# Three early loads of an attention kernel: issued from ScalarE's queue instead of SyncE's

## The chip, the cores and the metric

The kernel runs on one core of a Trainium2 chip. A core has a matrix engine (TensorE, PE in the profile, with its weight loads as PEld), three engines that work on tiles (VectorE or DVE, ScalarE or ACT, GpSimd or POOL) and SyncE (SP), which here only issues transfers between HBM and the on-chip memory. The engines run their own instruction streams and wait for one another through semaphores. The transfers are carried out by 16 DMA engines that all the queues share. The metric is the device time of one execution in microseconds, and the median of several runs is compared.

## The reference

```python
B, Sq, D = 8, 112, 640
H, Sk, Dh = 32, 512, 192
q = (x @ wq).reshape(B, Sq, H, Dh).transpose(0, 2, 1, 3)
scores = einsum("bhqd,bhkd->bhqk", q, k_cache) * Dh ** -0.5
p = softmax(scores, axis=-1)
o = einsum("bhqk,bhkd->bhqd", p, v_cache)
out = o.transpose(0, 2, 1, 3).reshape(B, Sq, H * Dh) @ wo
```

All arrays are bfloat16. `x` is 8 x 112 x 640 (1.15 MB), `wq` is 640 x 6144, `wo` 6144 x 640, and each cache is 8 x 32 x 512 x 192 (50 MB), so that some 117 MB have to be read.

## The kernel before

The work is cut into 64 units: 8 groups of 4 heads, and within a group the 8 batches. For each unit TensorE makes the scores of 4 heads (`do_S`, L949), ScalarE the exponentials (L1047), TensorE the products with v (`do_PV`, L967), VectorE and ScalarE normalise (L1112 to L1115, L1054), TensorE transposes the result (`do_T`, L978) and ScalarE stores it as the left side of the output projection (L1064). Between these, in slots that a table `slot` gives to each unit, TensorE makes the query projection of the next group and the output projection of the last one (`do_pair`, L928 and its helper L858).

Keys come as they lie in memory and are turned by VectorE in 32 x 32 blocks (`do_KT`, L1106), two units ahead. Three of every four value blocks are copied by GpSimd into a tile with a column of ones (`middle`, L1209). Query weights need another order of columns; GpSimd makes it (`reorder`, L1202). On GpSimd both stand in one list, written out by hand: for each unit first the weight chunk that is due, then a check of the softmax sums, then the copy of the values two units ahead.

The head of the program matters here. TensorE starts with 31 matmuls on zeros (`WARM`, L984 and L858), and then transposes `x` in 128-row blocks: `do_X(m)`, L854, five matmuls for each block. `x` is loaded in three pieces (`XM`): blocks 0 and 1, blocks 2 and 3, blocks 4 to 6; `do_X(0)` waits for the first piece, `do_X(2)` for the second, `do_X(4)` for the third. VectorE evacuates blocks 0 and 2 and part of 3 (L1134), ScalarE block 1 and the rest of 3 (L1023). Eight more matmuls on zeros (`BRIDGE`, L990 and L858) lie between the transposes and the first query projection. That one, `do_Q0_first` (L872), makes three column blocks of the first half of the rows and goes through the five 128-row chunks of the first query weights in order, waiting for each one's own semaphore `mW0[dc]`. Then come a fourth block (L892) and two blocks that read GpSimd's reordered copy (`do_Q0`, L887), blocks 4 to 6 of `x`, and the first unit's scores.

All loads are issued by SyncE in one list (`on_sync`), in this order: first piece of `x`, second piece of `x`, the five chunks of the first query weights (`load_wq(0, dc)`), keys of unit 0 (four transfers), third piece of `x`, and then keys, the second group's query weights, values and output weights. A load waits for its buffer where one is used again: three for keys, four for values. The issue of all loads is one line, L1309. ScalarE issues no loads. Its first instruction is the load of the table of activation functions (L1019, `ACT_TABLE_LOAD`), then a dummy exponential on one column, and then the evacuation of block 1 of `x`.

Of the kernel before, what the change touches and what calls it, by code (L numbers as in the profile page):

```python
# [666 lines left out]
def build_main(nc, x, k_cache, v_cache, wq, wo, out, flag, regs, hints):  # L667
    B, SQ, D = x.shape
    _, H, SK, DH = k_cache.shape
# [17 lines left out]
    WARM, WN, BRIDGE, RAW = 30, 25, 8, 4  # L687
    HINT_AT = {"act": 55, "dve": 54, "pool": 40, "sp": 56}
    NM = 2
    KP = [4] * NU  # L690
    PRE = 2 * 6
    EARLY_LOADS = ("k1", "q", "v0", "k2", "v1", "k3", "v2", "o")
# [68 lines left out]
    with ExitStack() as es:  # L761
# [58 lines left out]
        def W(eng, s, v):  # L820
            if v > 0:
                eng.wait_ge(s, v)
# [24 lines left out]
        def on_tensor(pe):  # L847
# [166 lines left out]
                do_pair(i, 1)  # L1014
            get_flag(pe)

        def on_scalar(act):
            W(act, vI, 1)
            act.activation(dmy[:, 1:2], dmy[:, 0:1], ACTF.Exp)  # L1019

            def evac_x(m, n=DC):
                W(act, pXT, m + 1)
                act.activation(xT[:, 0:n, 128 * m:128 * (m + 1)],  # L1023
                               psb[:, m, 0:128 * n].rearrange("p (c s) -> p c s", c=n), ACTF.Copy).then_inc(aX, 1)

            def evac(g, c, h):
                n = q_index[g, c, h]
                W(act, pQ, n + 1)
                if g >= 2 and c == 0 and h == 0:
                    W(act, pS, 4 * B * (g - 1))  # L1030
                act.activation(qT[g % 2][:, c, HQ * h:HQ * (h + 1)], ps[:, bank_of_Q0(n) if g == 0 else 6 + h, 0:HQ],  # L1031
                               ACTF.Copy).then_inc(aQ, 1)

            def evac_pair(i, j):
                if slot[i, j] and slot[i, j][0][0] == "Q" and slot[i, j][1] != FRONT:
                    for h in range(2):
                        evac(*slot[i, j][0][1:], h)

            def exp(u, a):
                W(act, pS, 4 * u + a + 1)  # L1040
                if a == 3 and u >= 2:
                    W(act, gM, u + 1)
                if a == 0:
                    W(act, pPV, u - 1)
                    if u < 2:
                        W(act, gV, 1)
                act.activation(pT[u % 2][:, a, :, 0:SQ], ps[:, a, 0:4 * SQ].rearrange("p (t q) -> p t q", t=4), ACTF.Exp,  # L1047
                               scale=scale).then_inc(aEX, 1)

            def norm(u):  # L1050
                W(act, vRC, u + 1)
                W(act, pT_, u - 1)
                for e in range(2):
                    ins = act.activation(os_[u % 2][:, DH * (2 + e):DH * (3 + e)], pv_of(u)[0:SQ, 1, e, 0:DH], ACTF.Copy,  # L1054
                                         scale=rinv[:, u % 4, 2 + e:3 + e])
                ins.then_inc(aNM, 1)

            def tevac(u):
                g, b = divmod(u, B)
                W(act, pT_, u + 1)  # L1060
                if g > 0:
                    W(act, pO, 2 * (MT * (g - 1) + (SQ * b + SQ - 1) // 128 + 1))
                src = psb[:, bank_of_T(u), 2:2 + 4 * RW].rearrange("p (k w) -> p k w", k=2)[:, :, 0:3 * SQ]
                act.activation(oT[:, :, SQ * b:SQ * (b + 1)].rearrange("p (k c) q -> p k c q", k=2),  # L1064
                               src.rearrange("p k (c q) -> p k c q", c=3), ACTF.Copy).then_inc(aT, 1)

            evac_x(1)
            evac_x(3, 2)
            for c in range(6):
                evac(0, c, 0)  # L1070
            for m in (4, 5):
                evac_x(m)
            for c in range(6):
                if c < 4:
                    exp(0, c)
                evac(0, c, 1)
            for i in range(1, NU + 2):
                if i == HINT_AT["act"]:
                    hints[mybir.EngineType.Activation] = act.mark_branch_hint_location()
                if i < NU:  # L1080
                    exp(i, 0)
                if i >= 2:
                    tevac(i - 2)
                if i < NU:
                    exp(i, 1)
                evac_pair(i, 0)
                if i < NU:
                    exp(i, 2)
                    exp(i, 3)
                if 1 <= i <= NU:  # L1090
                    norm(i - 1)
                evac_pair(i, 1)
            get_flag(act)
# [143 lines left out]
        def on_sync(sp):  # L1237
            loads = []

            def add(dst, src, s, count, waits):  # L1240
                loads.append((dst, src, s, count, waits))

            def load_x(j):
                m0, m1 = XM[j]
                add(xs[:, m0:m1, :], x.rearrange("b s d -> (b s) d")[128 * m0:128 * m1].rearrange("(m p) d -> p m d", p=128),
                    mX[j], 16, [])

            def load_wq(g, dc):
                src = wq[128 * dc:128 * (dc + 1), 4 * DH * g:4 * DH * (g + 1)]
                if g == 0:  # L1250
                    add(wqs[:, 0, dc, :], src, mW0[dc], 16, [])
                else:
                    add(wqr[:, dc, :], src, mWQ[dc], 16 * g, [(gW, DC * (g - 2) + dc + 1)])

            def load_wo(g, k):
                r0 = 4 * DH * g + 256 * k
                src = wo[r0:r0 + 256].rearrange("(p e) d -> p e d", e=2)
                for e in range(2):
                    add(wos[:, g % 2, 2 * k + e, :], src[:, e], mWO[g % 2][k], 32 * (g // 2 + 1),
                        [(pO, 2 * MT * (g - 1))])  # L1260

            def load_k(u):
                g, b = divmod(u, B)
                src = k_cache[b, 4 * g:4 * g + 4].rearrange("a (j s) d -> (a j) (s d)", s=16)
                for h in range(KP[u]):
                    cs = slice(16 // KP[u] * DH * h, 16 // KP[u] * DH * (h + 1))
                    add(kr[u % NK][:].rearrange("p s d -> p (s d)")[:, cs], src[:, cs], mK[u % NK], 16 * sum(KP[u % NK:u + 1:NK]),
                        [(vKT, 4 * (u - NK + 1))])

            def load_v(u):  # L1270
                g, b = divmod(u, B)
                for a in range(4):
                    add(vs[u % NV][:, a, 32:32 + 4 * DH], v_cache[b, 4 * g + a].rearrange("(m t) d -> m (t d)", t=4),
                        mV[u % NV], 64 * (u // NV + 1), [(pPV, u - NV + 1)])

            load_x(0)
            load_x(1)
            for dc in range(DC):
                load_wq(0, dc)
            load_k(0)  # L1280
            load_x(2)
            for step in EARLY_LOADS:
                for c in step[1:]:
                    {"k": load_k, "v": load_v}[step[0]](int(c)) if step[0] in "kv" else None
                if step[0] == "q":
                    for dc in range(DC):
                        load_wq(1, dc)
                if step[0] == "o":
                    for c in range(3):
                        load_wo(0, c)  # L1290
            for u in range(4, NU + 1):
                if u < NU:
                    load_k(u)
                if u - 1 >= 3:
                    load_v(u - 1)
                for g in range(2, NG):
                    d = u - max(4, 8 * (g - 1) - 6)
                    if 0 <= d < DC:
                        load_wq(g, d)
                for g in range(1, NG):  # L1300
                    d = u - (8 * g - 1)
                    if 0 <= d < 3:
                        load_wo(g, d)
            for n, (dst, src, s, count, waits) in enumerate(loads):
                if n == len(loads) - HINT_AT["sp"]:
                    hints[mybir.EngineType.SP] = sp.mark_branch_hint_location()
                for ws, wv in waits:
                    W(sp, ws, wv)
                sp.dma_start(dst, src).then_inc(s, 16)  # L1309
            parts = [(m, 0, D) for m in range(MT - 1)] + [(MT - 1, 0, HL), (MT - 1, HL, D)]  # L1310
            for n, (m, d0, d1) in enumerate(parts):
                W(sp, vO, 2 * (MT * (NG - 1) + m + 1) - (d1 == HL))
                sp.dma_start(out.rearrange("b s d -> (b s) d")[128 * m:128 * (m + 1), d0:d1], ob[:, m, d0:d1]).then_inc(mOUT[n], 16)
            get_flag(sp)
            for n in range(len(parts)):
                sp.wait_ge(mOUT[n], 16)
# [53 lines left out]
```

## Time and profile before

| what | value |
|---|---|
| median of 5 runs | 393.25 us (391.98 to 394.67) |
| the profiled execution's own time | 393.61 us |
| its span, first to last instruction | 391.9 us |
| TensorE busy | 386.1 us (99%) |
| VectorE, ScalarE, GpSimd busy | 283.8, 250.4, 152.7 us |
| read from HBM | 117.54 MB |
| moved by the DMA engines, mean | 306 GB/s |

The profile is of one execution. Its page gives the busy time of each engine, the span in 40 slices, and groups of instructions; the trace behind it answers for lines, waits and windows. A row of the timeline begins with the start and the duration in microseconds, then the engine, the line of the kernel, the operation, what it writes and reads, and how many instructions were merged; in brackets stands how long the engine was idle before and what ended that. A row of SyncE tells when transfers were issued, not when they landed. The DMA engines' share in the windows can be a little over 1, since packets overlap.

### The profile page before, as it was taken

Reading aid. Unit: us, or ns where it says so; the run is one execution under the profiler, and the core shown is the slowest. Engines: PE = TensorE matmul, PEld = TensorE weight load, DVE = VectorE, ACT = ScalarE, POOL = GpSimd, SP = SyncE. Lnnn points to the kernel's source line nnn. Section 1 sums busy time; section 2 is a strip of 40 time slices with the busy share of each in tenths; the row PEclk is TensorE's granted clock in tenths of the full one; section 3 lists DMA queues with packets and bytes.
Section 4 is the critical chain, followed back from the end, with each engine's and each line's share of the span. In section 5 each row is a group of like instructions: output and inputs, shape, how many; then the busy total and the mean of one; then the engine's idle time right before and its main releaser. Section 6 shows DMA issues by size and latency. Waiting matters only on the chain.

```text
span 391.9 us, 19834 instructions
## 1 busy us (share of the span) xinstructions
PE 386.1 (99%) x8865; PEld 243.2 (62%) x8262; DVE 283.8 (72%) x506; ACT 250.4 (64%) x550; POOL 152.7 (39%) x352
## 2 busy tenths in 40 slices
PE   8999988999999999999999999999999999999997
PEld 4555664756666656666665666665666666667664
DVE  1664786787896777776787766876778776789935
ACT  2767764766656765657746667557665667657662
POOL 5542444343443354334352354332553232333331
PEclk9999999999999999999999999999999999999999
DMA  8999999999999999989999999989899799999912
GB/s 268 377 362 317 331 330 355 348 363 333 331 358 366 319 315 355 296 281 300 329 344 310 283 318 318 345 283 309 263 335 333 229 302 302 321 302 293 304 48 70
DMA packets 88584, 120.00 MB, mean 306 GB/s; under 512 B 9776, under 2 KB 88496, under 8 KB 88496
## 3 DMA queue, kind: packets, MB, share of 16 engines
q1 hardware_dynamic: 88496, 118.72, 91.0%
q8 instruction: 68, 1.11, 1.2%
q14 instruction: 20, 0.16, 0.1%
HBM read 117.54 MB, written 1.15 MB: 303 GB/s over the span
## 4 chain that ended last, share of the span: by engine, by line
PE 96%; issue 1%; DMA 1%; POOL 1%; DVE 0%; ACT 0%; SPq 0%
PE ps L967 22%; PE ps L858 22%; PE ps L928 21%; PE ps L949 21%; PE ps L978 6%; PE ps L887 2%; PE ps L854 1%; DMA xs<-in_x_dram 1%; PE ps L872 1%; DMA vs<-in_v_cache_dram 0%; POOL vm L1209 0%; PE ps L892 0%; POOL wqs L1202 0%; DVE kt L1106 0%; DVE acc L1126 0%
## 5 line engine op out<-in xcount | busy, mean ns | idle before, releaser
L1106 DVE STREAM_TRANSPOSE kt<-kr 128x384 int32<-128x384 int32 x256 | 195.5, 872 | 12.5 <-DMA kr<-in_k_cache_dram 12.4
L1047 ACT ACTIVATE pT<-ps 128x448 bf16<-128x448 f32 x256 | 131.0, 561 | 84.4 <-PE ps L949 82.2
L949 PEld LDWEIGHTS ps<-qT,kt 32*128 32x128 bf16 x6144 | 77.0, 93 | 29.5 <-issue 20.2
L928 PE MATMUL ps<-wos,oT 128*128 128x320 bf16 (+2 forms) x342 | 92.9, 298 | 0.0
L967 PE MATMUL ps<-vm,pT 128*128 128x193 bf16 x768 | 91.5, 247 | 1.0 <-ACT oT L1064 0.8
L858 PE MATMUL ps<-wos,oT 128*128 128x320 bf16 (+1 forms) x340 | 91.3, 296 | 0.0
L949 PE MATMUL ps<-qT,kt 32*128 32x112 bf16 x6144 | 87.3, 208 | 0.4 <-DVE kt L1106 0.3
L1226 POOL TENSOR_SCALAR bad<-rinv 112x4 f32<-112x4 f32 x64 | 14.6, 228 | 187.1 <-DVE rinv L1112 186.9
L1209 POOL COPY vm<-vs 128x1152 int32<-128x1152 int32 x64 | 73.4, 1147 | 26.8 <-issue 19.9
L967 PEld LDWEIGHTS ps<-vm,pT 128*128 128x128 bf16 x768 | 67.9, 97 | 22.0 <-ACT oT L1064 11.7
L928 PE MATMUL ps<-xT,wqs 128*128 128x448 bf16 (+1 forms) x210 | 73.5, 350 | 1.0 <-POOL wqs L1202 1.0
L858 PE MATMUL ps<-xT,wqs 128*128 128x448 bf16 (+2 forms) x226 | 74.1, 341 | 0.0
L1054 ACT ACTIVATE os<-ps,rinv 112x192 bf16<-112x192 f32 x128 | 47.9, 436 | 26.7 <-DVE rinv L1112 26.7
L967 PE MATMUL ps<-vs,pT 128*128 128x193 bf16 x256 | 62.6, 245 | 0.0
L1031 ACT ACTIVATE qT<-ps 128x448 bf16<-128x448 f32 x96 | 47.8, 554 | 19.4 <-PE ps L928 13.5
L928 PEld LDWEIGHTS ps<-wos,oT 128*128 128x128 bf16 x342 | 33.2, 97 | 43.0 <-issue 35.9
L1129 DVE TENSOR_TENSOR acc<-ps,acc 128x320 f32<-128x320 f32 x84 | 37.3, 486 | 26.1 <-PE ps L928 25.9
L1064 ACT ACTIVATE oT<-ps 128x672 bf16<-128x672 bf16 x64 | 46.4, 725 | 2.1 <-PE ps L978 2.1
L1112 DVE RECIPROCAL rinv<-ps 112x4 f32<-112x4 f32 x64 | 11.1, 174 | 48.7 <-PE ps L967 48.7
L928 PEld LDWEIGHTS ps<-xT,wqs 128*128 128x128 bf16 x210 | 20.4, 97 | 35.4 <-issue 29.1
L1115 DVE TENSOR_TENSOR os<-ps,rinv 112x384 bf16<-112x384 f32 x64 | 35.7, 558 | 7.3 <-DVE rinv L1112 0.5
L1202 POOL COPY wqs<-wqr 128x384 bf16<-128x384 bf16 x70 | 33.2, 506 | 4.9 <-DMA wqr<-in_wq_dram 4.9
(44 smaller groups left out, 156.4 us busy)
## 6 DMA issues: line engine op xcount, KB each, us to landing
kr<-in_k_cache_dram SPq DMA_DIRECT2D x256, 192.0 KB, 4.0
vs<-in_v_cache_dram SPq DMA_DIRECT2D x256, 192.0 KB, 4.0
wos<-in_wo_dram SPq DMA_DIRECT2D x48, 160.0 KB, 4.1
wqr<-in_wq_dram SPq DMA_DIRECT2D x35, 192.0 KB, 4.7
wqs<-in_wq_dram SPq DMA_DIRECT2D x5, 192.0 KB, 4.1
out_dram<-xs SPq DMA_DIRECT2D x6, 160.0 KB, 1.8
xs<-in_x_dram SPq DMA_DIRECT2D x2, 320.0 KB, 3.3
xs<-in_x_dram SPq DMA_DIRECT2D x1, 480.0 KB, 5.9
```

Source lines behind the costliest of these rows:

```text
L858: return pe.add_instruction(mybir.InstMatmult(name=nc.get_next_instruction_name(), engine=mybir.EngineType.PE, ins=[pe.lower_ap_or_imm(rhs ...
L928: mm = (pe.matmul if h == hs[0] and f == 0 else held)(ps[:, bank_of(pair, h), cs], w, rhs[h][:, cs], q == 0, q == n - 1 and f == cuts - 1)
L949: mm = pe.matmul(ps[:, a, SQ * t:SQ * (t + 1)], kt[u % NT][p, t, c // 2, :, c % 2], qT[g % 2][p, c, SQ * b:SQ * (b + 1)], start=(c == 0), ...
L967: mm = pe.matmul(pv[:, k, e, 0:DH + 1], pT[u % 2][:, a, t, :], src[:, a, v0:v0 + DH + 1], start=(t == 0), stop=(t == 3), skip_group_check= ...
L1031: act.activation(qT[g % 2][:, c, HQ * h:HQ * (h + 1)], ps[:, bank_of_Q0(n) if g == 0 else 6 + h, 0:HQ], ACTF.Copy).then_inc(aQ, 1)
L1047: act.activation(pT[u % 2][:, a, :, 0:SQ], ps[:, a, 0:4 * SQ].rearrange("p (t q) -> p t q", t=4), ACTF.Exp, scale=scale).then_inc(aEX, 1)
L1054: ins = act.activation(os_[u % 2][:, DH * (2 + e):DH * (3 + e)], pv_of(u)[0:SQ, 1, e, 0:DH], ACTF.Copy, scale=rinv[:, u % 4, 2 + e:3 + e])
L1064: act.activation(oT[:, :, SQ * b:SQ * (b + 1)].rearrange("p (k c) q -> p k c q", k=2), src.rearrange("p k (c q) -> p k c q", c=3), ACTF.Co ...
L1106: dve.transpose(dst, src).then_inc(vKT, 1)
L1115: dve.tensor_tensor(os_[u % 2][:, 0:2 * DH].rearrange("p (e d) -> p e d", e=2), pv[0:SQ, 0, :, 0:DH], rinv[:, u % 4, 0:2][:, :, None].broa ...
L1129: ins = dve.tensor_tensor(ob[:, m, cs] if g == NG - 1 else acc[:, m, cs], src, acc[:, m, cs], op=ALU.add)
L1209: gp.tensor_copy(vm[u % NM][:].rearrange("p a (t w) -> p a t w", w=RW)[:, :, :, 0:DH].bitcast(I32), vs[u % NV][:, :, 32:32 + 3 * DH].rearr ...
```

## The change

ScalarE issues three of the loads at its very start, ahead of the table load: the second piece of `x` (320 KB) and chunks 1 and 3 of the first query weights (192 KB each). SyncE's list loses these three; it now begins with the first piece of `x`, chunks 0, 2 and 4, the keys of unit 0. Two helper functions give the source of a piece and of a chunk. Semaphores, sizes, destinations and the waits of those who read the data are the same, and TensorE's, VectorE's and GpSimd's instructions keep their order.

```diff
+    ACT_W0 = (1, 3)
...
+        def x_piece_src(j):
+            m0, m1 = XM[j]
+            return x.rearrange("b s d -> (b s) d")[128 * m0:128 * m1].rearrange("(m p) d -> p m d", p=128)
+
+        def wq_src(g, dc):
+            return wq[128 * dc:128 * (dc + 1), 4 * DH * g:4 * DH * (g + 1)]
+
         def on_scalar(act):
+            act.dma_start(xs[:, XM[1][0]:XM[1][1], :], x_piece_src(1)).then_inc(mX[1], 16)
+            for dc in ACT_W0:
+                act.dma_start(wqs[:, 0, dc, :], wq_src(0, dc)).then_inc(mW0[dc], 16)
             W(act, vI, 1)
             act.activation(dmy[:, 1:2], dmy[:, 0:1], ACTF.Exp)
...
             load_x(0)
-            load_x(1)
             for dc in range(DC):
-                load_wq(0, dc)
+                if dc not in ACT_W0:
+                    load_wq(0, dc)
             load_k(0)
             load_x(2)
```

More of the change, by code (lines that the diff above doesn't have):

```diff
@@ L1244, in load_x @@
                 m0, m1 = XM[j]
-                add(xs[:, m0:m1, :], x.rearrange("b s d -> (b s) d")[128 * m0:128 * m1].rearrange("(m p) d -> p m d", p=128),
-                    mX[j], 16, [])
+                add(xs[:, m0:m1, :], x_piece_src(j), mX[j], 16, [])
             def load_wq(g, dc):
-                src = wq[128 * dc:128 * (dc + 1), 4 * DH * g:4 * DH * (g + 1)]
+                src = wq_src(g, dc)
                 if g == 0:
```

## Prediction

> **What bounds the kernel now.** I began with the page (span, busy times, DMA row).
>
> ```profile
> span 391.9 us, 19834 instructions
> PE 386.1 (99%) x8865; PEld 243.2 (62%) x8262; DVE 283.8 (72%) x506; ACT 250.4 (64%) x550; POOL 152.7 (39%) x352
> ...
> DMA  8999999999999999989999999989899799999912
> ```
>
> TensorE is busy 386.1 of 391.9 us, so a change at the head can only matter through TensorE's few idle moments. The DMA row is as full as TensorE's, so the second question is whether transfers pace TensorE anywhere. The list of waits of TensorE over the whole span has five entries, all short; besides the two shown (who, for whom: us, times, longest) there are 1.0 us before the first warm-up matmul, 0.3 for a key transpose at 55 us and 0.2 for x:
>
> ```profile
> PE ps L928 <- POOL wqs L1202: 1.0, 1, 1.0
> PE ps L967 <- ACT oT L1064: 0.8, 1, 0.8
> ```
>
> Then the head, in order of time (start, duration, engine, line):
>
> ```profile
> 0.73 1.28 ACT L1019 ACT_TABLE_LOAD   x1 [0.73 <-PEq L1355]
> 0.74 0.95 SPq L1309 DMA_DIRECT2D xs<-in_x_dram  x2
> 1.74 2.36 SPq L1309 DMA_DIRECT2D wqs<-in_wq_dram  x5
> 3.93 2.29 PE L854 MATMUL ps<-ident,xs 128*128 128x128 bf16 x20 [0.17 <-DMA xs<-in_x_dram]
> 5.19 0.70 ACT L1023 ACTIVATE xT<-ps 128x640 bf16<-128x640 bf16 x1 [2.96 <-PE ps L854]
> 5.91 4.54 POOL L1202 COPY oT<-wqs 128x384 bf16<-128x384 bf16 x10 [3.50 <-DMA wqs<-in_wq_dram]
> 6.52 2.09 SPq L1309 DMA_DIRECT2D kr<-in_k_cache_dram  x4
> 6.84 3.02 PE L872 MATMUL ps<-xT,wqs 128*32 128x448 bf16 x60
> 8.65 2.89 SPq L1309 DMA_DIRECT2D wqr<-in_wq_dram  x5
> 10.74 2.07 PE L887 MATMUL ps<-xT,oT 128*128 128x448 bf16 x10
> ```
>
> The only transfer that TensorE waits for here is the first piece of x: issued at 0.74, landed 3.05 us later (3.79), transposes from 3.93. The second piece, issued at 1.23, takes 3.5 us to land (4.7). Its ten transposes come behind the first ten, which at 2.29/20 = 0.11 us each last until about 5.0, so nothing waits for it. The five weight chunks, issued 0.47 us apart from 1.74 and landing after 4.0 to 4.1 us, are in by 7.8; the projection (6.84, five steps of 3.02/5 = 0.6 us) wants the last at 9.2, and GpSimd, which starts on the first at 5.91, is through at 10.45, before TensorE's reordered columns at 10.74. **None of the three transfers that move is late today.**
>
> The windows view tells how full the transfers are (the last two numbers: DMA share and GB/s):
>
> ```profile
> 1.50:2.00 0.50, 0.50 (x10) 0.00 (x0) 0.00 (x0) 0.50 (x1) 0.50 (x5) 1.00 0.39 41
> 2.00:2.50 0.50, 0.50 (x10) 0.00 (x0) 0.00 (x0) 0.22 (x2) 0.35 (x8) 1.00 0.67 141
> 2.50:4.00 1.50, 1.33 (x18) 0.10 (x3) 0.00 (x0) 0.00 (x0) 0.00 (x0) 1.00 0.98 352
> 12.00:26.00 14.00, 14.00 (x273) 8.50 (x263) 8.66 (x14) 10.31 (x22) 7.06 (x14) 1.00 1.07 375
> ```
>
> From 2.5 us on the DMA engines are full. SyncE's own rows run end to start from 0.74 to 66 us, never more than 0.45 us apart, so up to there its stream waits for no buffer and hence not for TensorE. Where does that stream meet TensorE? In the chain between 58 and 67 us:
>
> ```profile
> 59.48 1.47 DMA vs<-in_v_cache_dram
> 60.95 3.56 issue
> 64.51 1.15 POOL vm L1209
> 65.65 0.91 POOL wqs L1202 x2
> 66.61 0.36 PE ps L928
> ```
>
> A piece of v issued at 59.48 lands 4.9 us later (64.4). GpSimd, idle till then, copies it (1.15), reorders a weight chunk (0.91), and only then TensorE goes on at 66.61, after the 1.0 us wait listed above. The chain's link from that piece back to a value product at 59.34 is an inference I do not follow: the buffer was freed by the fifth product, at about 48.6. So at 66.6 us the schedule is set by transfers and TensorE has **1.0 us in hand**. After that it shows no wait that the list counts.
>
> **The change, part by part.**
>
> *Off SyncE's queue:* three issues, (1.74 - 1.23) + 2 x 0.47 = 1.45 us. First weight chunk up by 0.51 us, third by 0.98, fifth and everything behind by 1.45. But the transfers were full already, and SyncE shows it: four k issues at 6.52 take 2.09 and five at 8.65 take 2.89, 0.52 and 0.58 each against 0.47 in the first weight rows. It is being held back. Being ahead only brings it to that brake sooner; the bytes ahead of any later piece stay the same. Bounds for the stream: later by nothing that a row shows, earlier by at most 1.45 us. I take 0, by the nearest row (share 0.98 to 1.07). What two queues might win is the ramp: 0.5 us at 141 instead of 352 GB/s and 0.5 at 41 are (211 + 311) x 0.5 / 352 = 0.74 us of transfer at the utmost, and most of that is latency that a second queue has too.
>
> *Onto ScalarE:* three issues at 0.43 to 0.51 each (SyncE's rows; ScalarE has none). Table load 0.73 to about 2.15, done 3.45, dummy exponential (0.20) 3.65; first real work at 5.19. Cost 0; cover 1.5 us. Even at SyncE's slowest early row, 1.06 us, it would end at 0.73 + 3.18 + 1.28 + 0.20 = 5.4, 0.2 late, and the next paragraph moves that work later too. Nobody waits for the dummy.
>
> *The second piece of x now starts with the first.* Both are 320 KB and issued together at 0.74 into full engines. The first piece loses its head start. Bounds for its landing: 3.79 (unchanged, if ScalarE's queue gets going late) and 4.7 (where the second lands now; the two together hold the same bytes). Two equal transfers served in turn end nearly together, so I take 4.5, nearer the upper end: +0.7 us. Transposes, their evacuations and the projection follow with unchanged durations, so TensorE starts the projection at about 7.5 instead of 6.84. [...] No row here shows two load queues at work.
>
> *Weight chunks:* the pairs (0, 1) and (2, 3) arrive together, so the first may land at the second's time, about 0.5 us later (6.3). The projection wants it at 7.5. GpSimd ends at up to 10.95 instead of 10.45, while its reader moves from 10.74 to 11.4. Cost 0; cover 0.45 us, the same as today less 0.05 to 0.3.
>
> *Sum:* TensorE +0.7 us from 4 to 66 us; there it finds 1.0 us of waiting for v, which swallows it: +0.7 - 0.7 + 0 (stream) = 0. The wait shrinks to about 0.3. Profiled execution: 393.6 us (span 391.9 and 1.7 around it), after: 393.6. It stands 0.36 above the median 393.25 of runs that spread over 2.7 us; the forecast against the median is **393.3**. Where the cover would be gone: each further 0.1 us at the head beyond 1.0 costs 0.1.
>
> **Rivals.**
>
> 1. *Slower: the array's full speed comes later.* Matmuls run at half pace first (20 transposes of 128 columns 0.11 us each; later 448 columns in 3.02/15 = 0.20), and the pace steps up just before the projection, some 5.6 us after the first warm-up matmul at 0.99. Warm-up ends at about 3.76 and today leaves a hole of 0.17 us; mine is 0.9. If that restarts the count, full pace comes at about 4.7 + 5.6 = 10.3 instead of 6.6; 3.7 us at half pace lose up to 1.85. Head 0.7 + 1.85 = 2.55, less the 1.0 of cover: +0.2 to +1.5, 394.4 likely. It decides from a head delay over 1.0. For it: the hole lies in the middle of the warm-up. Against: TensorE would still be busy three quarters of that stretch. [...]
> 2. *Faster: the stream keeps part of its 1.45 us.* v lands earlier and the wait at 66 shrinks from both sides: at most -0.3 with a head 0.7 late, at most -1.0 with an unharmed head; 392.6. For it: shares of 0.98 and a DMA rate of 316 GB/s between 26 and 42 us. Against: SyncE's braked rows above.
> 3. *Nothing happens:* ScalarE's issues reach the engines late, x lands as now: 393.3, the same time by another way.
> 4. *Slower: two queues disturb each other* and the stream itself falls behind; every us lost before 64.4 is a us at the end. No row prices it; by the 1.07 against 0.98 share, some 0.5 to 2 us.
>
> **How the numbers follow.** Main case 0.52, rival 1 0.20, rival 2 0.10, rival 3 0.10, rival 4 0.08. Half a per cent is 2.0 us, about what this kernel's measurement tells from none. No case's middle lies beyond it; the upper ends of 1 and 4 and the spread of the runs put 0.14 above, that spread and what I have not seen 0.09 below, 0.77 within. Range: rival 2's end, 392.2, to rival 1's upper end with some spread, 395.0.
>
> **What would show it.** In the changed profile: ScalarE's table load from about 2.2; the first piece of x landing near 4.5 and transposes starting there (right), or at 3.9 (rival 3); projection at 7.5 with five steps of 0.6 (right) or 1.1 (rival 1); TensorE's wait for GpSimd near 66 us at about 0.3 instead of 1.0, ending at the same 66.6. It is wrong if that wait keeps its size or the point moves by over 0.5 us.

## The result

The changed kernel takes 394.38 us, median of 52 runs, against 393.07 for 94 runs of the kernel before. The ratio is **1.0026, with a 95% interval of 1.0016 to 1.0036**: about 1.0 us slower (the medians themselves lie 1.3 us apart; the ratio is not their quotient). The interval leaves out 1, so the loss is real, but it is inside the half per cent that the forecast called no change, and inside its range. But the forecast's likeliest case said 393.3. The time that came is that of its first rival, 394.4, to which it gave 2 chances in 10.

The page of the changed kernel's profile (execution of 394.24 us):

```profile
span 392.5 us, 19834 instructions
...
PE 386.9 (99%) x8865; PEld 243.3 (62%) x8262; DVE 284.2 (72%) x506; ACT 250.3 (64%) x550; POOL 152.8 (39%) x352
...
q1 hardware_dynamic: 87936, 118.00, 90.7%
...
q10 hardware_dynamic: 560, 0.72, 0.5%
```

The new queue, q10, carries 560 packets and 0.72 MB, just the three moved loads. The span grew by 0.6 us from one profiled execution to the other. The head, in order of time:

```profile
0.74 0.49 ACTq L1026 DMA_DIRECT2D xs<-in_x_dram  x1
1.25 0.98 ACTq L1028 DMA_DIRECT2D wqs<-in_wq_dram  x2
2.26 1.28 ACT L1030 ACT_TABLE_LOAD   x1 [2.26 <-issue]
4.84 2.29 PE L855 MATMUL ps<-ident,xs 128*128 128x128 bf16 x20 [1.08 <-DMA xs<-in_x_dram]
7.92 3.91 PE L873 MATMUL ps<-xT,wqs 128*32 128x448 bf16 x60
12.71 2.06 PE L888 MATMUL ps<-xT,oT 128*128 128x448 bf16 x10
```

Three readings. The transposes start at 4.84 instead of 3.93, after a wait of 1.08 us for x (0.17 before). Their duration, 2.29, is the same. But the first projection now takes 3.91 us instead of 3.02, and the reordered columns (L888) start at 12.71 instead of 10.74: the head is **1.97 us** late, 0.91 of it from x and 1.06 from a slower array. The windows show the slower array (columns: window, its length, busy time and count for PE and the others, clock, DMA share, GB/s):

```profile
6.60:9.60 3.00, 3.00 (x33) 1.13 (x28) 0.85 (x2) 0.59 (x2) 3.00 (x8) 1.00 1.07 382
9.80:12.00 2.20, 2.20 (x52) 1.18 (x48) 2.09 (x2) 0.49 (x2) 0.53 (x2) 1.00 1.07 370
26.00:42.00 16.00, 16.00 (x376) 9.77 (x357) 10.07 (x17) 12.31 (x28) 5.95 (x14) 1.00 1.07 372
```

33 matmuls in 3.0 us, then 52 in 2.2. The first window also holds short matmuls from before the projection; the weight loads inside the projection show the step cleanly:

```profile
9.01 0.16 PEld L873 LDWEIGHTS ps<-xT,wqs 128*32 128x32 bf16 x4 [0.22 <-issue]
9.39 0.16 PEld L873 LDWEIGHTS ps<-xT,wqs 128*32 128x32 bf16 x4 [0.22 <-issue]
9.76 1.63 PEld L873 LDWEIGHTS ps<-xT,wqs 128*32 128x32 bf16 x36 [0.22 <-issue]
```

Four of them each 0.37 us, then 36 in a row, four each 0.19. TensorE was busy all the time, at half pace until about 9.8. The clock column stays at 1.00 in both windows, so it cannot be trusted for this stretch; the spacing can. The third line of the windows matters further down: between 26 and 42 us the loads now run at 372 GB/s, where the first profile of the kernel before had 316:

```profile
26.00:42.00 16.00, 16.00 (x386) 9.35 (x361) 9.95 (x16) 12.01 (x28) 4.77 (x11) 1.00 0.99 316
```

And the waits of TensorE over the whole span:

```profile
PE ps L855 <- DMA xs<-in_x_dram: 1.1, 1, 1.1
PE ps L985 <- DVE wt L1107: 1.0, 1, 1.0
PE ps L968 <- ACT oT L1075: 0.8, 1, 0.8
PE ps L950 <- DVE kt L1117: 0.3, 1, 0.3
```

The wait for GpSimd's weights near 66 us, 1.0 us before, is gone. So the sum of the two profiles is +1.97 at the head and -1.37 from there to the end, which is the +0.60 of the span. Compared matmul by matmul, 1.15 us come back exactly where that wait was (the matmul at 66.61 before starts at 67.48, where the one ahead of it is 2.02 late). Another 0.35 come back near 365 us; there the second and third profiles of the kernel before gain as much on the first, so that part belongs to the first profile and not to the change.

### The profile page after: what moved, and what is told of

It is laid out like the page before. It is cut to its first block, busy times and chain, and to the rows that moved or that the text cites. A ratio compares the mean times of both kernels' runs of the same rounds, so it can differ in the third digit from the quotient of the medians.

```text
span 392.5 us, 19834 instructions
## 1 busy us (share of the span) xinstructions
PE 386.9 (99%) x8865; PEld 243.3 (62%) x8262; DVE 284.2 (72%) x506; ACT 250.3 (64%) x550; POOL 152.8 (39%) x352
## 3 DMA queue, kind: packets, MB, share of 16 engines
HBM read 117.54 MB, written 1.15 MB: 302 GB/s over the span
## 4 chain that ended last, share of the span: by engine, by line
PE 97%; DMA 1%; DVE 0%; ACT 0%; issue 0%
PE ps L968 22%; PE ps L859 22%; PE ps L929 22%; PE ps L950 21%; PE ps L979 6%; PE ps L888 2%; DMA xs<-in_x_dram 1%; PE ps L873 1%; PE ps L855 1%; PE ps L893 0%; DVE kt L1117 0%; DVE acc L1137 0%; ACT oT L1075 0%; ACT pT L1058 0%; DVE xs L1140 0%
## 5 line engine op out<-in xcount | busy, mean ns | idle before, releaser
L968 PEld LDWEIGHTS ps<-vm,pT 128*128 128x128 bf16 x768 | 67.9, 97 | 22.1 <-ACT oT L1075 11.6
L1123 DVE RECIPROCAL rinv<-ps 112x4 f32<-112x4 f32 x64 | 11.1, 174 | 51.9 <-PE ps L968 51.9
```

The source lines that it names most:

```text
L968: mm = pe.matmul(pv[:, k, e, 0:DH + 1], pT[u % 2][:, a, t, :], src[:, a, v0:v0 + DH + 1], start=(t == 0), stop=(t == 3), skip_group_check= ...
```

## The experiments

Each ratio below is against runs of the kernel before on the same chip. The theory after this: the second piece of x takes the engines from the first; TensorE stands idle for 1.1 us in the middle of its warm-up; that idle stretch, the hole, puts off the array's full pace; and the delay is only partly taken back later. The rivals: that full pace comes when it comes, and one profile proves nothing; that the weight chunks or the second queue cost by themselves; and, for what is taken back, that the wait near 66 us was chance.

**e1_x_only** is the changed kernel with the piece of x alone moved.

```diff
-    ACT_W0 = (1, 3)
+    ACT_W0 = ()
```

> Of the change only one part: the second piece of x on ScalarE's queue, all five weight chunks back on SyncE's. Theory (x pieces side by side): the first piece lands at about 4.7 as in the changed kernel, TensorE waits 1.1 us for it, the array's full pace comes later in many runs, and the time is the changed kernel's, +0.6 to +1.3 us over before (ratio 1.0015 to 1.0033). Rival (the weight chunks in pairs are what costs): first piece at 3.8 to 4.2 and the time within 0.3 us of before.

Measured: 394.26 us (12 runs), ratio 1.0040 (1.0013 to 1.0067), the changed kernel's loss.

```profile
4.79 2.29 PE L855 MATMUL ps<-ident,xs 128*128 128x128 bf16 x20 [1.03 <-DMA xs<-in_x_dram]
7.87 3.71 PE L873 MATMUL ps<-xT,wqs 128*32 128x448 bf16 x60
```

The first piece landed at 4.65, the hole is 1.0 us, the projection is slow again. The weight chunks are not needed for the loss.

**e4_hole** leaves the loads of the kernel before and only shortens the warm-up, so that the same hole arises.

```diff
-    WARM, WN, BRIDGE, RAW = 30, 25, 8, 4
+    WARM, WN, BRIDGE, RAW = 19, 25, 8, 4
```

> The kernel before, loads untouched, with 20 instead of 31 warm-up matmuls, which leaves the changed kernel's hole of about 1.1 us ahead of the transposes. Theory: full pace comes late as in the changed profile (near 9.7 us or later, half of the projection at half pace), TensorE reaches 54 us 1.0 to 1.8 us later, but the loads land as before, so that its wait near 66 us swallows up to 1.0: time +0.1 to +0.8 us (1.0003 to 1.002). Rival (no effect of the hole): full pace near 6.6, wait near 66 us 1.0 us, time within 0.2 us of before.

Measured: 394.29 us, ratio 1.0035 (1.0009 to 1.0060).

```profile
3.92 2.29 PE L854 MATMUL ps<-ident,xs 128*128 128x128 bf16 x20 [1.08 <-DMA xs<-in_x_dram]
7.00 3.75 PE L872 MATMUL ps<-xT,wqs 128*32 128x448 bf16 x60
```

x is on time, and still the projection takes 3.75 us. A hole alone, with no queue touched, costs as much as the change (the intervals overlap). The median lost more than the 0.1 to 0.8 expected (1.4 us, interval 0.35 to 2.4), so less of the delay is swallowed than I still believed then.

**e3_more_warm** and **e9_changed_warm36** fill the hole in the changed kernel, wholly and by half.

```diff
-    WARM, WN, BRIDGE, RAW = 30, 25, 8, 4
+    WARM, WN, BRIDGE, RAW = 42, 25, 8, 4     # e3_more_warm
+    WARM, WN, BRIDGE, RAW = 36, 25, 8, 4     # e9_changed_warm36
```

> The changed kernel with 43 instead of 31 warm-up matmuls, so that the hole before the first transposes (1.1 us) is filled. Theory (the hole postpones full pace): full pace at the projection's start or before, five steps of 0.6 us; TensorE then is 0.9 us late from x alone and the earlier loads have removed its 1.0 us wait: time within 0.3 us of before, 0.8 to 1.2 us under the changed kernel (ratio to before 0.999 to 1.001). Rival (full pace depends on chance, not on the hole): still +0.7 to +1.3 us over before (1.0018 to 1.0033).

> The changed kernel with 37 instead of 31 warm-up matmuls: half of the hole is filled, some 0.55 us is left. [...] Rival (the loss is the late x alone and grows with its delay): as the changed kernel, since x lands as late.

Measured: 392.56 us, ratio 0.9986 (0.9963 to 1.0008), and 392.83 us, ratio 1.0000 (0.9982 to 1.0018). First e3_more_warm, then e9_changed_warm36:

```profile
4.93 1.50 PE L855 MATMUL ps<-ident,xs 128*128 128x128 bf16 x20 [0.17 <-DMA xs<-in_x_dram]
7.00 3.02 PE L873 MATMUL ps<-xT,wqs 128*32 128x448 bf16 x60
```

```profile
4.87 2.21 PE L855 MATMUL ps<-ident,xs 128*128 128x128 bf16 x20 [0.61 <-DMA xs<-in_x_dram]
7.60 3.02 PE L873 MATMUL ps<-xT,wqs 128*32 128x448 bf16 x60
```

x lands as late as in the changed kernel (4.79 and 4.74), and **the loss is gone**. With the hole filled, full pace comes already during the transposes (1.50 instead of 2.29). With 0.6 us left of it, full pace comes just before the projection, the head is 0.76 us late (reordered columns at 11.50), and the time is that of the kernel before, as the forecast's likeliest case had it. (The interval of e9 reaches 1.0018 and so just touches that of the changed kernel; that of e3 lies below it.) So a hole of 0.6 us was borne and one of 1.0 to 1.1 was not, in the profiles and in the medians.

The moment of full pace, read from the spacing of the matmuls, wanders from profile to profile even without a long hole: in the eleven profiles whose holes are at most 0.7 us it comes between 4.3 us (e5_w_after_x, below) and 6.9 us (e9, and the second profile of the kernel before). In the three with a hole of 1.0 to 1.1 us it comes at 8.5 (e4), 9.3 (e1) and 9.8 (changed). It is the gap between the two groups, and not any single profile, that speaks against the rival of chance.

**e2_w_behind_table** was to move only weight chunks, out of the way of x. Against the changed kernel:

```diff
-            act.dma_start(xs[:, XM[1][0]:XM[1][1], :], x_piece_src(1)).then_inc(mX[1], 16)
+            W(act, vI, 1)
+            act.activation(dmy[:, 1:2], dmy[:, 0:1], ACTF.Exp)
             for dc in ACT_W0:
                 act.dma_start(wqs[:, 0, dc, :], wq_src(0, dc)).then_inc(mW0[dc], 16)
-            W(act, vI, 1)
-            act.activation(dmy[:, 1:2], dmy[:, 0:1], ACTF.Exp)
...
             load_x(0)
+            load_x(1)
```

> The other part alone, and moved so that it cannot touch x: both first pieces of x on SyncE, chunks 1 and 3 issued by ScalarE behind its table load and dummy exponential (from about 2.3 us). Theory that SyncE's issuing paces the loads between 28 and 66 us: SyncE is two issues (0.95 us) ahead, v of unit 8 lands 1 us or more before 64.4, TensorE's 1.0 us wait near 66 us shrinks to 0 to 0.3, x lands at 3.8, and the time is 0.5 to 1.0 us under before (ratio 0.9974 to 0.9987). Rival (the DMA engines pace them, and the earlier landing in the changed profile was chance): wait stays, time within 0.3 us of before.

Measured: 393.87 us, ratio 1.0016 (0.9989 to 1.0044), open either way. It did not do what it was made for:

```profile
0.74 1.28 ACT L1027 ACT_TABLE_LOAD   x1 [0.74 <-PEq L1365]
...
1.01 0.87 ACTq L1029 DMA_DIRECT2D wqs<-in_wq_dram  x2
...
4.38 1.07 PE L855 MATMUL ps<-ident,xs 128*128 128x128 bf16 x10 [0.63 <-DMA xs<-in_x_dram]
...
6.17 0.73 PE L855 MATMUL ps<-ident,xs 128*128 128x128 bf16 x10 [0.72 <-DMA xs<-in_x_dram]
```

The loads stand behind the table load in the program, but were issued at 1.01, while it ran, and so fell among the pieces of x: two holes, 0.63 and 0.72, neither as long as 1.0, and the later transposes at full pace.

**e5_w_after_x** made ScalarE wait for the first piece of x and took chunks 3 and 4, both pieces of x on SyncE. Against the changed kernel:

```diff
-    ACT_W0 = (1, 3)
+    ACT_W0 = (3, 4)
...
-            act.dma_start(xs[:, XM[1][0]:XM[1][1], :], x_piece_src(1)).then_inc(mX[1], 16)
+            W(act, vI, 1)
+            act.activation(dmy[:, 1:2], dmy[:, 0:1], ACTF.Exp)
+            W(act, mX[0], 16)
             for dc in ACT_W0:
                 act.dma_start(wqs[:, 0, dc, :], wq_src(0, dc)).then_inc(mW0[dc], 16)
-            W(act, vI, 1)
-            act.activation(dmy[:, 1:2], dmy[:, 0:1], ACTF.Exp)
...
             load_x(0)
+            load_x(1)
```

> Only weight chunks moved, and without touching x: both first pieces of x on SyncE, ScalarE waits for the first piece's landing and then issues chunks 3 and 4. Theory (x side by side and the hole are the whole loss): first piece lands at 3.8, no wait longer than 0.3 us before the transposes, first projection starts 0.8 us after the last transpose, chunks in before they are read; time within 0.4 us of before (ratio 0.999 to 1.001). Rival 1 (a head start of SyncE's stream is worth something in an ordinary execution): 0.5 to 1.0 us under before (0.9974 to 0.9987). Rival 2 (a second load queue costs by itself): 0.5 to 1.3 us over (1.0013 to 1.0033).

Measured: 394.67 us, ratio 1.0036 (1.0013 to 1.0058). None of the three cases: the chunks came too late.

```profile
3.87 0.86 ACTq L1030 DMA_DIRECT2D wqs<-in_wq_dram  x2
...
9.24 0.75 PE L873 MATMUL ps<-xT,wqs 128*32 128x448 bf16 x12 [1.31 <-DMA wqs<-in_wq_dram]
...
10.68 0.97 PE L873 MATMUL ps<-xT,wqs 128*32 128x448 bf16 x12 [0.69 <-DMA wqs<-in_wq_dram]
```

Issued at 3.87 and 4.29 on an otherwise empty queue, they landed at 9.2 and 10.6, in line with the keys that SyncE had issued at 3.66 and 4.14 (8.3 and 9.8). The trace's packets show where the time went: the first packet of ScalarE's queue starts at 6.54, 2.7 us after its issue (1.65 in the changed kernel). TensorE stood for 2.0 us, and here the windows show the half pace in their clock column too:

```profile
4.30:11.00 6.70, 4.58 (x83) 2.28 (x77) 1.40 (x4) 1.04 (x2) 4.02 (x9) 1.00 0.98 330
11.10:14.40 3.30, 3.30 (x31) 1.21 (x24) 2.75 (x4) 1.96 (x4) 0.54 (x2) 0.50 1.07 382
14.50:20.00 5.50, 5.50 (x130) 3.72 (x129) 3.12 (x5) 3.59 (x7) 4.08 (x10) 1.00 1.07 374
```

An array already at full pace (36 matmuls of the projection in 1.89 us) fell back to half after two holes of 1.3 and 0.7 (0.50 in the clock column from 11.1 to 14.4 us), though it was busy all through that stretch. This is a toll of the same kind as in the changed kernel, seen from the other side. It was recorded in three of the twelve runs only, this one among them (mean clock 0.996), and they are the three slowest.

**e7_before_look2** and **e8_before_look3** are the kernel before, unchanged, profiled twice more.

> The kernel before once more, unchanged, for its profile. Theory (the 1.0 us wait of TensorE for GpSimd near 66 us was in that one execution): no such wait, v of unit 8 lands before 64.0, and the span is the end of the first projection's fifth step plus 381 us. Rival (it belongs to the kernel, and is the cover of the prediction): wait of 0.8 to 1.2 us near 66 us again, span plus 382.

> The same once more. Theory: no wait near 66 us in at least one of the two looks. Rival: the wait in both.

Measured: executions of 392.65 and 394.44 us. The waits of TensorE in the second profile, then the first two lines of the third:

```profile
PE ps L984 <- DVE wt L1096: 1.0, 1, 1.0
PE ps L967 <- ACT oT L1064: 0.8, 1, 0.8
PE ps L949 <- DVE kt L1106: 0.3, 1, 0.3
```

```profile
PE ps L928 <- POOL wqs L1202: 1.3, 1, 1.3
PE ps L984 <- DVE wt L1096: 1.0, 1, 1.0
```

**The wait near 66 us is absent in one profile and 1.3 us in the other.** Both sides of the expectation hold in part: the wait is neither chance in a single execution nor a fixed cover.

**e11_before_warm36, e6_before_warm42, e10_before_warm54** and a repeat, **e12_before_warm42_again**, delay the transposes of the kernel before with a longer warm-up and no hole.

```diff
-    WARM, WN, BRIDGE, RAW = 30, 25, 8, 4
+    WARM, WN, BRIDGE, RAW = 36, 25, 8, 4     # or 42, or 54
```

> The kernel before with 37 warm-up matmuls, which end at about 4.3 at half pace: no hole, transposes 0.2 to 0.4 us later. Theory: the small hole of 0.17 us in the kernel before costs nothing, and the delay is swallowed or regained: within 0.4 us of before (0.999 to 1.001). [...]

> The kernel before, loads untouched, with 43 instead of 31 warm-up matmuls: the transposes start 0.9 us later with no hole ahead of them, as in e3_more_warm, which has the changed loads. [...] Rival (the moved loads are what made e3_more_warm fast): 0.6 us or more slower than e3_more_warm, +0.5 to +1.0 over before.

> e6_before_warm42 once more, on the same chip as the two other warm-up lengths. If its 0.8 us (0.9979) was real: 0.9970 to 0.9990 again, and a look without the late stalls of the first profile. If it was the spread of the runs: within 0.3 us of before.

> The kernel before with 55 warm-up matmuls: TensorE is kept busy until 5.1 to 5.7 us, so the transposes start 1.2 to 1.8 us late without a hole. Theory (head delays come through once the wait near 66 us is used up): GpSimd's reordered columns are reached 0.5 to 1.2 us after those of e6_before_warm42, no wait near 66 us, what follows them 380 us; time +0.2 to +1.0 us over before (1.0005 to 1.0025). Rival (delays at the head are always swallowed): within 0.2 us of before.

Measured: 37 matmuls 392.74 us, ratio 0.9995 (0.9982 to 1.0009); 43 matmuls 392.66, 0.9979 (0.9960 to 0.9998), and again 393.15, 1.0007 (0.9992 to 1.0023); 55 matmuls 393.57, 1.0016 (1.0003 to 1.0030). The gain of the first run with 43 did not come back, so it is no faster version, and e3_more_warm, whose interval holds 1, is none either. Nor does it matter whether loads were moved: filled up with 43 warm-up matmuls, both kernels take about the time of the kernel before. With 55:

```profile
5.55 1.87 PE L854 MATMUL ps<-ident,xs 128*128 128x128 bf16 x20
...
11.89 1.31 PE L887 MATMUL ps<-xT,oT 128*128 128x448 bf16 x6
```

The head is 1.15 us late by this profile (11.89 against 10.74), the median 0.6 us (interval 0.1 to 1.2). Here a head delay without hole or moved loads comes through by about half; how much in one execution depends on stalls such as this one, from the repeat with 43:

```profile
PE ps L928 <- DVE acc L1129: 0.9, 1, 0.9
```

Put together, one profile of each (us; "rest" is the span less the start of the reordered columns; v8 is the landing of the last piece of v of unit 8, its issue plus its time to landing):

| run | first x lands | wait for x | reordered columns start | rest | v8 | ratio |
|---|---|---|---|---|---|---|
| before, three profiles | 3.8, 3.7, 3.8 | 0.2, 0, 0.2 | 10.7, 10.8, 10.4 | 381.1, 380.1, 382.3 | 64.4, 63.4, 64.5 | 1 |
| changed | 4.7 | 1.1 | 12.7 | 379.7 | 61.3 | 1.0026 |
| e1_x_only | 4.7 | 1.0 | 12.5 | 380.1 | 62.8 | 1.0040 |
| e9_changed_warm36 | 4.7 | 0.6 | 11.5 | 379.8 | 61.3 | 1.0000 |
| e3_more_warm | 4.8 | 0.2 | 10.9 | 379.8 | 63.4 | 0.9986 |
| e2_w_behind_table | 4.3 | 0.6 + 0.7 | 11.4 | 379.9 | 63.6 | 1.0016 |
| e5_w_after_x | 3.9 | 0.2 | 13.5 | 380.1 | 61.7 | 1.0036 |
| e4_hole | 3.8 | 1.1 | 11.6 | 380.3 | 64.0 | 1.0035 |
| e11_before_warm36 | 3.8 | 0 | 10.8 | 380.1 | 63.8 | 0.9995 |
| e6, e12 (43) | 3.9, 3.8 | 0, 0 | 10.5, 10.8 | 382.9, 381.3 | 64.1, 63.2 | 0.9979, 1.0007 |
| e10_before_warm54 | 3.8 | 0 | 11.9 | 380.2 | 64.0 | 1.0016 |

In the six profiles with loads moved off SyncE the rest is 379.7 to 380.1, mean 379.9; in the eight without, 380.1 to 382.9, mean 381.0, and only there does TensorE wait for weights or for VectorE's accumulation after 60 us. v8 lands at 62.3 on average with moved loads and at 63.9 without, and between 26 and 42 us the loads run at 363 to 372 GB/s in each of the six and at 316 to 350 in each of the eight. So the moved issues do bring later loads forward, on average by 1.6 us, but by 0.4 to 2.7 in single profiles and not in step with what was moved (0.5 us of issuing in e1, 0.95 in e2 and e5, 1.45 in the others). That this saves about 1 us of late stalls is a tendency only: five of the six also have a late head, and a late head alone takes the wait away (e4 and e10, loads not moved, show none). No run isolated it, since both tries to move the weight chunks alone (e2, e5) failed as tests.

## Why the prediction was right or wrong

*The half per cent and the range:* right. No case was worth 2 us, and none came. The bar is wide, though: the middle of every case that the forecast listed lies inside it, so the bar does not tell them apart, and by the forecast's own sign (the point at 66.6 us moving by over 0.5; it moved by 0.88) the likeliest case was wrong.

*"The second piece of x now starts with the first":* right in kind, and the size was at the upper end that I gave (4.7 measured, 4.5 taken); e1 shows it alone. That the two would be served in turn was my assumption, for which the profile of before had no row; the packets of the trace agree with it: from 3.0 to 6.5 us of the changed profile SyncE's queue moved 618 KB and ScalarE's 673, and from 7 to 9 us of e5's 311 and 315. ScalarE's queue began later (first packets at 2.39 against 1.82, both issued at 0.74), and the first piece landed just ahead of the second (4.71 and 5.01).

*"Onto ScalarE" and "Weight chunks":* right. The table load ran from 2.26 to 3.54, TensorE never waited for a chunk, and e1 without the moved chunks loses as much as the whole change (the intervals overlap). The first chunk even landed at 5.6, not 6.3. One remark there does not come out: a cover of 0.45 us is more than today's 0.29 (10.45 to 10.74), not less; nothing rested on it.

*The pace of the array, put aside into rival 1:* here the likeliest case failed. It had the projection follow "with unchanged durations", and the reason against the rival was "TensorE would still be busy three quarters of that stretch". Three quarters was not enough: with a hole of 1.1 us half pace lasted to about 9.8 and cost 1.06 us. e4 shows the hole alone to be sufficient, and e3 and e9 show that filling it, or half of it, removes the loss. Rival 1 had the mechanism (a long hole puts off full pace: 8.5 to 9.8 us in the three profiles with one, at most 6.9 in the others), the place and the final number, its head delay of 2.55 being 1.97 in the profile. Its count of 5.6 us after the first warm-up matmul was one sample: without a long hole the profiles give 3.3 to 5.9.

*"... earlier by at most 1.45 us. I take 0":* wrong for the loads. The nearest row, braked issues in the first 12 us, was the wrong place to look; the stretch that counts is 26 to 42 us, where the engines moved 316 to 350 GB/s in every profile with the loads left on SyncE and 363 to 372 in every one with loads moved. The rival quoted the 316 and the sum ignored it. v8 landed 3.1 us earlier than in the first profile, 2.8 before the mean of the three (64.1), beyond the bound of 1.45. What sets the rate there was not settled; between 10 and 66 us of the first profile nine of SyncE's issues take 1.1 to 1.8 us instead of 0.43, each starting within 0.4 us of a 16 KB instruction fetch in the trace, and the forecast did not count them. For the time of this profile the 0 did no harm: TensorE came to the point at 66.6 us only at 67.48, when in the first profile too GpSimd was through (66.56).

*"1.0 us in hand":* half right. In the changed profile and in those of e1, e4, e9 and e10, all with a late head, about 1.15 us come back at that point against the first profile, with and without moved loads, as the forecast had reckoned. But the cover was read from one execution. Two more profiles gave waits of 0 and 1.3, so there is not always something to give back, and e4 lost more in the median than a cover of 1.0 would leave (0.9 us late at the head, 1.4 lost, at least 0.35).

So the right total of the first rival came from a head delay that was 0.6 smaller and a recovery that was 1.37 rather than 1.0 in this profile. That its time agrees with the median to 0.02 us is luck; the mechanism is not.

## What to carry to other kernels

A transfer that nobody waits for can still do harm when it is issued earlier, if it then shares the engines with the one that everybody waits for (here the first piece of x landed at 4.7 us instead of 3.8). Ask of every wait at a kernel's start not only how long it is, but whether it interrupts the matrix engine's warm-up: here 0.6 us of idling cost nothing that could be measured and 1.1 us cost another microsecond, and six or twelve more dummy matmuls bought it back. A slack of a microsecond read from one profile is a sample; take two or three profiles before building a forecast on it.

## What the runs showed that I had not expected

- The clock column can read 1.00 over a stretch in which matmuls run at half pace (33 in 3.0 us against 52 in 2.2, weight loads 0.37 us apart); where half pace was recorded (0.50 in e5) the spacing is the same 0.37.
- Loads on ScalarE's queue were issued at 1.01 while that engine's table load ran from 0.74 to 2.02: standing behind it in the program did not hold them back. In e5, where ScalarE also waited for the first piece of x, the first was issued at 3.87.
- An otherwise empty second queue gave two loads no advantage: issued at 3.87 and 4.29, they took 5.3 and 6.3 us to land, among SyncE's loads of the same moments (4.6 and 5.6 us). Its packets started 2.7 us after the issue, and only then did the queues share the engines evenly (315 KB against 311 from 7 to 9 us).
- The same kernel, 43 warm-up matmuls, measured 0.9979 (0.9960 to 0.9998) and then 1.0007 (0.9992 to 1.0023): a fifth of a per cent with an interval that just leaves out 1 was not yet a finding.
